# Attention and two gated layers on one core: the written-out order of instructions is made with later transfers, longer vector steps and new priorities

## The chip, the cores and the metric

The kernel runs on one core of a Trainium2 chip. The metric is the device time of one execution in microseconds, lower is better; three runs of the kernel before are given.

## What is computed

Block-causal attention over 4 batches, 8 heads, 576 positions and 64 features, then two layers of two products each, with an elementwise function between them. In the first layer the function is h * cos(h), in the second relu(h) squared.

```python
def _attn_ref(q, k, v):
    ...
    scores = scale * np.matmul(q, k.transpose(0, 1, 3, 2))
    mask = block_i >= block_j
    scores = np.where(mask, scores, -1000000000.0)
    scores = scores - np.max(scores, axis=-1, keepdims=True)
    attn = np.exp(scores)
    attn = attn / (np.sum(attn, axis=-1, keepdims=True) + 1e-09)
    return np.matmul(attn, v)
...
h = x @ w_in          # 2304 x 512 by 512 x 2048
g = h * np.cos(h)     # second layer: np.maximum(h, 0) ** 2
x = g @ w_out         # 2304 x 2048 by 2048 x 512
```

q, k and v are float32. The four weight matrices are 64-bit floats, so the kernel loads their 8-byte words and makes float32 of them itself.

## The kernel before

**The work.** The matmuls take float32 operands split in a high part (rounded for the matmul) and a low part (the rest); each product is then three matmuls: high by high, high by low, low by high (`mm3`). The high parts come from `hi_part`, the low parts from `lo_part`.

**The stages.** First attention by units of one batch and one pair of heads (`attention`: load, transposes of q and k in `prep`, scores, softmax, transposes of the result, product with v), together with the first half of the first layer's columns (`first_in`, `in_cos`, `first_out`) for groups of 256 and 320 tokens. Then three stages over chunks of 512 tokens (four chunks and a half one): the second half of the first layer, and the two halves of the second layer. Each chunk's input comes back from DRAM (tile x, from x_d or y_d, in `raw_rows`), sums of its quarters (tiles t) are made in `load_quarters`, and high and low parts xh and xl in `x_parts`. These stages multiply 256 x 256 blocks with seven products instead of eight (`quad`); the weights' seven combinations are made in `left_parts` (high and low part so, from ws or c), stored to DRAM as wi_d and loaded back as w in `factors`. The sums of products are kept in PSUM or in tiles p, u and r; the function's result is split into gh and gl, the operands of the second product (`y`). The results of half a layer go to DRAM (y1_d, y_d, y2_d) and are added in with the other half.

**The weights.** `weight_piece` (line 683) loads 128 x 512 words into a tile raw, of which there are two (`RAWS`, L694). ACT makes tiles t and c of their top bytes, DVE or POOL subtracts them, and DVE puts the middle bytes in (L430). This last step frees raw.

**The order.** Nothing is ordered by hand. Each step is recorded with a cost in ns, the tiles that it reads and writes, and the engines that may do it (`FREE` names the kinds with a choice: hi, lo, copy, norm, abs, wt, eps, add). `Recorder.schedule` (line 219) then plays the program through. Among the steps that are ready at an engine's free time, it takes the one with the lowest priority number, which is the step's place in the program plus an offset by kind and phase (`PUT_OFF`). A step with a choice goes to the engine that would end it first, with that engine's cost changed by a factor 1 + `BIAS` of the phase. Phase 0 is the first batch, phase 1 the other batches, phase 2 the second half of the first layer, phase 3 the second layer. The order that comes out is what each engine gets; on the chip it then works through it strictly in that order, waiting where an operand is not there yet.

Transfers are an engine of their own in it (`DMA`, issued from SP's queue, 500 ns apart): a transfer lands at line 319, and its readers are ready 50 ns later by line 328:

```python
o.end = landed = max(t + self.LANDING, landed) + o.service   # LANDING = 1750; service = size / 420, 2400 for raw
...
lat = 50 if e == "DMA" else self.LAT.get((e, a), 0 if a == e else 100)
```

The other handovers take `LAT`, 87 to 258 ns by pair of engines. On the chip a semaphore guards each of them, so the order has no bearing on what is computed.

Of the kernel before, what the change touches and what calls it, by code (L numbers as in the profile page):

```python
# [21 lines left out]

BANKS = {"h": 1, "y": 1, "s": 2, "t": 1, "a": 1}, {"h": 6, "y": 3, "s": 5, "t": 3, "a": 1}

BIAS = [{"DVE": 1.84, "ACT": 0.4, "POOL": 0.23}, {"DVE": 3.3, "ACT": -0.66, "POOL": -0.23}, {"DVE": 0.9, "ACT": -3.04, "POOL": -0.02}, {"DVE": -0.14, "ACT": -3.34, "POOL": 1.15}]

FREE = {"hi": "POOL ACT", "lo": "DVE POOL", "copy": "ACT DVE", "norm": "POOL DVE", "abs": "DVE", "wt": "POOL DVE", "eps": "ACT DVE", "add": "DVE POOL"}

# [8 lines left out]
NATB = 1  # L37


PUT_OFF = [{"load": -35, "weights": -24, "prep": 14, "scores": 25, "weighted": 9, "split": 279, "in": -32, "cos": -170, "out": -10, "warm": 9160, "later": 935}, {"load": 376, "weights": -150, "prep": -70, "scores": 69, "weighted": -156, "split": 84, "in": 43, "cos": -141, "out": -21, "later": 886}, {"load": 194, "weights": 721, "prep": 429, "scores": 43, "weighted": -280, "split": 374, "in": -36, "cos": -108, "out": -53, "later": 567}, {"in": 32, "out": 14, "later": 22}]  # L40

UPTO = [8, 12, 14, 16, 18]
NEG = -1000000000.0
# [10 lines left out]
class View:  # L54
    def __init__(self, vt, chain, ix, halves):
        self.vt, self.chain, self.ix, self.halves = vt, chain, ix, halves
# [83 lines left out]
class Recorder:  # L140
# [6 lines left out]
    }  # L147

    ISSUE, LANDING = 500, 1750

    def __init__(self):
        self.ops = []
# [18 lines left out]
    def any(self, alts, writes=(), reads=(), after=(), lat=0, holds=()):  # L171
# [6 lines left out]
        o.phase, o.kind = self.phase, self.kind  # L178
        o.prio = o.seq + PUT_OFF[self.phase].get(self.kind, 0)
        o.deps, o.outs, o.tiles = set(after), [], []  # L180
# [38 lines left out]
    def schedule(self):  # L219
        ops = self.ops  # L220
        engines = dict.fromkeys(e for o in ops for e in o.alts)
        for o in ops:
            for t in o.tiles:
                o.deps.update(getattr(t.pool, "after", ()))
                if t.banks is None and t.before is not None:
                    o.deps.update(t.before.users)
            o.ahead -= o.deps
            o.ahead.discard(o)
            o.left, o.ready = len(o.deps) + len(o.ahead), dict.fromkeys(o.alts, 0.0)
            for d in o.deps:  # L230
                d.outs.append(o)
            for d in o.ahead:
                d.behind.append(o)
        free = dict.fromkeys(engines, 0.0)
        free["DMA"] = 1850.0
        waiting = {e: [] for e in engines}
        ready = {e: [] for e in engines}

        def wait(o, at=0.0):
            for e in o.alts:  # L240
                heapq.heappush(waiting[e], (max(at, o.ready[e]), o.prio, o.seq))

        def finish(o, e, t):

            at = max(t, free[e], o.ready[e])
            at += sum(ops[s].alts[e][1] for p, s in ready[e] if p < o.prio and e in ops[s].alts)
            if e == "DVE" and len(o.alts[e]) > 3 and pool[1]:
                at = max(at, pool[0])
            return at + o.alts[e][1] * (1 + BIAS[o.phase][e])

        for o in ops:
            if not o.left:
                wait(o)
        order, done, gives, table, cold, busy = [], 0, [], None, True, 0.0
        pool, landed, ended = (0.0, False), 0.0, 0.0
        while done < len(ops):

            best = None
            for e in free:
                t = free[e]  # L260
                if not ready[e] and waiting[e]:
                    t = max(t, waiting[e][0][0])
                elif not ready[e]:
                    continue
                if best is None or t < best[0]:
                    best = (t, e)
            if gives and (best is None or gives[0][0] <= best[0]):
                at, _, _, x = heapq.heappop(gives)
                x.banks.give(x.tag, x.bank)
                for o in x.banks.blocked:  # L270
                    wait(o, at)
                x.banks.blocked = []
                continue
            t, e = best
            while waiting[e] and waiting[e][0][0] <= t:
                _, p, s = heapq.heappop(waiting[e])
                heapq.heappush(ready[e], (p, s))
            _, s = heapq.heappop(ready[e])
            o = ops[s]
            free[e] = max(free[e], t)  # L280
            if e not in o.alts:
                continue
            if len(o.alts) > 1:
                a = min(o.alts, key=lambda a: (finish(o, a, t), a != e))
                o.alts = {a: o.alts[a]}
                if a != e:
                    continue
            new = [x for x in o.tiles if x.banks is not None and x.bank is None]
            full = next((x.banks for x in new if not x.banks.fits(x.tag, len(new))), None)
            if full is not None:  # L290
                full.blocked.append(o)
                continue
            for x in new:
                x.bank = x.banks.take(x.tag)
            o.eng, o.cost, o.fn = o.alts[e][:3]
            o.port = o.alts[e][3] if len(o.alts[e]) > 3 else 0
            o.alts = {}
            if o.table and o.table != table:
                t, table = t + 1283, o.table
            if e == "PE":  # L300

                if t - ended > 2300:
                    cold = True
                if t - ended > 250:
                    busy = t
                if t - busy > 3400:
                    cold = False
                if cold:
                    o.cost *= 2
            if o.port and e == "DVE" and t < pool[0] and (pool[1] or o.port == 2):  # L310
                t = pool[0]
            o.begin = t
            o.end = t + o.cost
            if e == "PE":
                ended = o.end
            if e == "POOL":
                pool = (o.end, bool(o.port))
            if e == "DMA":
                o.end = landed = max(t + self.LANDING, landed) + o.service
            if o.hook:  # L320
                o.hook()
            free[e] = o.begin + self.ISSUE if e == "DMA" else o.end
            order.append(o)
            done += 1
            for x in o.outs:
                x.left -= 1
                for a in x.alts:
                    lat = 50 if e == "DMA" else self.LAT.get((e, a), 0 if a == e else 100)
                    x.ready[a] = max(x.ready[a], o.end + lat)
                if not x.left:  # L330
                    wait(x)
            for x in o.behind:
                x.left -= 1
                for a in x.alts:
                    x.ready[a] = max(x.ready[a], o.begin)
                if not x.left:
                    wait(x)
            for x in o.tiles:
                if x.banks is not None:
                    x.todo = getattr(x, "todo", len(x.users)) - 1  # L340
                    x.last = max(getattr(x, "last", 0.0), o.end)
                    if not x.todo:
                        heapq.heappush(gives, (x.last + 100, x.users[0].seq, x.bank, x))
        order.sort(key=lambda o: (o.begin, o.seq))
        return order
# [1067 lines left out]
```

## Time and profile before

| | us |
|---|---|
| median of 3 runs | 1039.64 |
| lowest and highest | 1037.94, 1040.03 |
| the profiled execution | 1038.25 |
| its span, first to last instruction | 1036.5 |

The profile is that of one execution. Its engines: PE is TensorE's matmuls, PEld its weight loads, DVE VectorE, ACT ScalarE, POOL GpSimd, SP the engine that issues all transfers. L and a number is a line of the kernel. A busy time is the union of the records of one engine; a wait is idle time of an engine, put down to the semaphore that came last. PEclk is the granted clock of TensorE as a share of 2.4 GHz; a transfer's time runs from issue to landing. In out<-in the names are those of the program's tiles.

### The profile page before, as it was taken

What the parts mean: (1) busy time and instruction counts of PE and PEld (TensorE: products, weight loads), DVE (VectorE), ACT (ScalarE), POOL (GpSimd) and SP (SyncE); (2) the same over time, 40 slices, a digit from 0 to 9 for tenths busy, and PEclk for the clock granted to TensorE, in tenths of its full rate; (3) what the DMA queues carried; (4) which work ended last, traced back from release to release, by engine and by line L of the source; (5) the groups of instructions that cost most, each with busy time, mean ns of one, the idle gap of its engine ahead of it and who ended that gap; (6) DMA issues with size and microseconds to landing.
All of it is one profiled execution on the core that took longest, in us unless ns stands there. A gap on an engine that the chain in (4) does not pass through costs nothing.

```text
span 1036.5 us, 18463 instructions
## 1 busy us (share of the span) xinstructions
PE 990.8 (96%) x6672; PEld 863.7 (83%) x6672; DVE 641.0 (62%) x1344; ACT 636.4 (61%) x1417; POOL 340.6 (33%) x412
## 2 busy tenths in 40 slices
PE   7779999999999999999999889999998999999998
PEld 5557887878888898989797779898987888988987
DVE  4765666666364446395897688856868285736432
ACT  7897678878898975464484747545655272504301
POOL 5584144567886766060664520000000000000000
PEclk8989999999999999999999999999999999999999
DMA  6644133455565375712445698315474553221111
GB/s 181 186 134 125 47 84 86 133 170 154 150 186 175 111 264 180 269 41 89 141 147 169 200 304 308 98 49 193 163 214 163 226 201 102 62 82 51 52 61 41
DMA packets 136507, 150.11 MB, mean 145 GB/s; under 512 B 70368, under 2 KB 102624, under 8 KB 136416
## 3 DMA queue, kind: packets, MB, share of 16 engines
q1 hardware_dynamic: 136416, 148.93, 45.6%
q8 instruction: 53, 0.87, 0.4%
q14 instruction: 38, 0.31, 0.1%
HBM read 99.09 MB, written 49.81 MB: 144 GB/s over the span
## 4 chain that ended last, share of the span: by engine, by line
PE 54%; DMA 15%; ACT 10%; POOL 8%; DVE 8%; issue 4%; SPq 0%; POOLq 0%; ACTq 0%; DVEq 0%
PE y L529 24%; PE h L529 18%; PE t L546 5%; DMA wi_d<-so 5%; PE a L539 4%; DMA x<-y_d 3%; PE s L539 2%; POOL xl L467 2%; DMA raw<-in_moe_w_in_dram 2%; DMA w<-wi_d 2%; POOL e L512 2%; ACT gh L453 2%; DMA x<-x_d 2%; DVE r L423 1%; ACT e L414 1%
## 5 line engine op out<-in xcount | busy, mean ns | idle before, releaser
L529 PE MATMUL h<-xh,w 128*128 128x256 f32 x1536 | 289.8, 284 | 5.0 <-ACT p L482 2.8
L529 PEld LDWEIGHTS h<-xh,w 128*128 128x128 f32 x1536 | 244.5, 192 | 9.1 <-ACT p L482 3.8
L529 PE MATMUL y<-gh,w 128*128 128x256 f32 (+2 forms) x832 | 213.6, 334 | 13.6 <-ACT gh L453 8.4
L529 PE MATMUL h<-xl,w 128*128 128x256 f32 x768 | 217.3, 283 | 0.0
L529 PE MATMUL y<-w,gh 128*128 128x512 f32 x576 | 185.0, 398 | 2.6 <-ACT gh L453 2.6
L529 PEld LDWEIGHTS y<-gh,w 128*128 128x128 f32 x832 | 144.0, 191 | 29.5 <-ACT gh L453 10.7
L529 PEld LDWEIGHTS h<-xl,w 128*128 128x128 f32 x768 | 147.4, 192 | 1.1
L529 PE MATMUL y<-gl,w 128*128 128x256 f32 (+2 forms) x416 | 136.4, 332 | 3.7 <-POOL gl L467 3.5
L529 PEld LDWEIGHTS y<-w,gh 128*128 128x128 f32 x576 | 107.9, 189 | 29.1 <-ACT gh L453 4.2
L453 ACT ACTIVATE gh<-r 128x512 fp32r<-128x512 f32 (+2 forms) x134 | 74.4, 558 | 67.2 <-DVE r L1291 32.5
L529 PE MATMUL y<-w,gl 128*128 128x512 f32 x288 | 113.6, 397 | 0.0
L956 DVE CUSTOM_DVE_ANT_0 e<-s,mask 128x384 f32<-128x384 f32 (+4 forms) x160 | 70.9, 479 | 43.9 <-PE s L539 36.6
L512 POOL TENSOR_SCALAR e<-e,st 128x384 f32<-128x384 f32 (+4 forms) x134 | 83.4, 637 | 44.1 <-DVE st L977 31.7
L529 PEld LDWEIGHTS y<-gl,w 128*128 128x128 f32 x416 | 79.3, 191 | 12.0 <-POOL gl L467 5.4
L414 ACT ACTIVATE e<-e,st 128x128 f32<-128x128 f32 (+4 forms) x144 | 82.9, 578 | 6.3 <-DVE st L956 4.2
L471 DVE TENSOR_TENSOR gl<-r,gh 128x512 fp32r<-128x512 f32 (+2 forms) x88 | 65.8, 752 | 15.0 <-ACT gh L453 11.8
L546 PE MATMUL t<-ident,e 128*128 128x128 f32 (+1 forms) x400 | 66.8, 284 | 7.5 <-POOL e L512 7.1
L423 DVE TENSOR_TENSOR o<-y,y 128x512 f32<-128x512 f32 (+1 forms) x38 | 25.1, 662 | 72.9 <-PE y L529 69.1
L467 POOL TENSOR_TENSOR gl<-r,gh 128x256 fp32r<-128x256 f32 (+2 forms) x60 | 56.2, 938 | 37.9 <-ACT gh L453 37.2
L482 ACT ACTIVATE p<-h 128x512 f32<-128x512 f32 x48 | 28.3, 589 | 64.2 <-PE h L529 64.2
L529 PEld LDWEIGHTS y<-w,gl 128*128 128x128 f32 x288 | 54.5, 189 | 13.8 <-DVE gl L471 1.1
L482 ACT ACTIVATE r<-t 128x384 f32<-128x384 f32 (+1 forms) x111 | 56.9, 532 | 13.0 <-PE t L546 12.0
(140 smaller groups left out, 1881.5 us busy)
## 6 DMA issues: line engine op xcount, KB each, us to landing
wi_d<-so SPq DMA_DIRECT2D x84, 256.0 KB, 2.7
w<-wi_d SPq DMA_DIRECT2D x42, 512.0 KB, 6.8
raw<-in_moe_w_in_dram SPq DMA_DIRECT2D x32, 512.0 KB, 5.2
raw<-in_moe_w_out_dram SPq DMA_DIRECT2D x32, 512.0 KB, 3.9
y<-y_d SPq DMA_DIRECT2D x34, 256.0 KB, 3.0
y_d<-o SPq DMA_DIRECT2D x34, 256.0 KB, 3.0
x<-y_d SPq DMA_DIRECT2D x16, 512.0 KB, 3.9
k<-in_k_dram SPq DMA_DIRECT2D x36, 128.0 KB, 3.0
```

The source lines that it names most:

```text
L414: return nc.scalar.activation(real(out), real(in_), func, **kw)
L423: out.size / 0.96 + 68, lambda: nc.vector.tensor_tensor(real(out), real(a), real(b), op=op), [out], [a, b],
L453: "ACT": ("ACT", n / 1.2 + 92, lambda: nc.scalar.activation(real(hi), real(x), ACTF.Copy)),
L467: lambda: nc.gpsimd.tensor_tensor(real(lo), real(x), real(f(hi)), op=ALU.subtract), 1,
L471: lambda: nc.vector.tensor_tensor(real(lo), real(x), real(f(hi)), op=ALU.subtract), 1,
L482: "ACT": ("ACT", n / 1.2 + 50, lambda: nc.scalar.activation(real(out), real(ps), ACTF.Copy)),
L512: lambda: nc.gpsimd.tensor_scalar(real(out), real(x), real(s), 1.0, op0=ALU.mult, op1=ALU.mult),
L529: lambda: nc.tensor.matmul(real(ps), lhsT=real(lhsT), rhs=real(rhs), start=start, stop=stop, skip_group_check=True),
L539: nc.tensor.matmul(real(ps), lhsT=real(l), rhs=real(r), start=start, stop=stop, skip_group_check=True)
L546: lambda: nc.tensor.transpose(real(out), real(in_), real(ident)[0:rows, 0:rows]), [out], [in_, ident],
L956: lambda: nc.vector.tensor_tensor_reduce(out=real(e), in0=real(ps), in1=real(m), scale=-1.0, scalar=BIG, op0=ALU.add, op1=ALU.min, accum_o ...
```

## The change

Three numbers are new in the order's model: the readers of a transfer are ready 2497 ns after line 319's landing instead of 50, every step on DVE, ACT or POOL takes 16 ns more, and every handover between two engines 4 ns more. All offsets (`PUT_OFF`) but three are new, and so are all twelve biases. No step, tile, buffer or cost formula is changed.

```diff
--- before.py
+++ after.py
@@ -22,7 +22,7 @@
 
 BANKS = {"h": 1, "y": 1, "s": 2, "t": 1, "a": 1}, {"h": 6, "y": 3, "s": 5, "t": 3, "a": 1}
 
-BIAS = [{"DVE": 1.84, "ACT": 0.4, "POOL": 0.23}, {"DVE": 3.3, "ACT": -0.66, "POOL": -0.23}, {"DVE": 0.9, "ACT": -3.04, "POOL": -0.02}, {"DVE": -0.14, "ACT": -3.34, "POOL": 1.15}]
+BIAS = [{"DVE": 1.89, "ACT": 0.46, "POOL": 0.26}, {"DVE": 2.58, "ACT": -0.56, "POOL": 0.68}, {"DVE": -0.3, "ACT": -2.99, "POOL": 0.29}, {"DVE": -1.17, "ACT": -3.72, "POOL": 2.36}]
 
 FREE = {"hi": "POOL ACT", "lo": "DVE POOL", "copy": "ACT DVE", "norm": "POOL DVE", "abs": "DVE", "wt": "POOL DVE", "eps": "ACT DVE", "add": "DVE POOL"}
 
@@ -37,7 +37,7 @@
 NATB = 1
 
 
-PUT_OFF = [{"load": -35, "weights": -24, "prep": 14, "scores": 25, "weighted": 9, "split": 279, "in": -32, "cos": -170, "out": -10, "warm": 9160, "later": 935}, {"load": 376, "weights": -150, "prep": -70, "scores": 69, "weighted": -156, "split": 84, "in": 43, "cos": -141, "out": -21, "later": 886}, {"load": 194, "weights": 721, "prep": 429, "scores": 43, "weighted": -280, "split": 374, "in": -36, "cos": -108, "out": -53, "later": 567}, {"in": 32, "out": 14, "later": 22}]
+PUT_OFF = [{"load": 114, "weights": -25, "prep": 11, "scores": 21, "weighted": -156, "split": 287, "in": 62, "cos": -140, "out": -54, "warm": 9160, "later": 877}, {"load": 381, "weights": -104, "prep": -71, "scores": 69, "weighted": -789, "split": 92, "in": 43, "cos": -127, "out": -24, "later": 911}, {"load": 543, "weights": 771, "prep": 52, "scores": 520, "weighted": 66, "split": 1698, "in": 0, "cos": -391, "out": -77, "later": 696}, {"in": 92, "out": 124, "later": -317}]
 
 UPTO = [8, 12, 14, 16, 18]
 NEG = -1000000000.0
@@ -147,6 +147,7 @@
     }
 
     ISSUE, LANDING = 500, 1750
+    LATE, SLACK, EXTRA = 2497, 4, 16
 
     def __init__(self):
         self.ops = []
@@ -310,7 +311,7 @@
             if o.port and e == "DVE" and t < pool[0] and (pool[1] or o.port == 2):
                 t = pool[0]
             o.begin = t
-            o.end = t + o.cost
+            o.end = t + o.cost + (self.EXTRA if e in ("DVE", "ACT", "POOL") else 0)
             if e == "PE":
                 ended = o.end
             if e == "POOL":
@@ -325,7 +326,7 @@
             for x in o.outs:
                 x.left -= 1
                 for a in x.alts:
-                    lat = 50 if e == "DMA" else self.LAT.get((e, a), 0 if a == e else 100)
+                    lat = self.LATE if e == "DMA" else self.LAT.get((e, a), 0 if a == e else 100) + (self.SLACK if a != e else 0)
                     x.ready[a] = max(x.ready[a], o.end + lat)
                 if not x.left:
                     wait(x)
```

## Rows read from the trace of the kernel before

**Rows 1.** The page's busy time, share of the span and instructions by engine
```profile
PE 990.8 (96%) x6672; PEld 863.7 (83%) x6672; DVE 641.0 (62%) x1344; ACT 636.4 (61%) x1417; POOL 340.6 (33%) x412
```

**Rows 2.** Busy time by stage: length, each engine, clock, DMA share, GB/s
```profile
0.00:104.00 104.00, 83.93 (x566) 62.43 (x567) 62.10 (x188) 84.37 (x209) 63.27 (x83) 0.93 0.59 156
104.00:390.00 286.00, 283.15 (x2225) 242.17 (x2224) 161.23 (x533) 241.71 (x642) 172.63 (x248) 1.00 0.48 143
390.00:520.00 130.00, 124.64 (x790) 114.43 (x789) 84.96 (x104) 67.77 (x128) 54.05 (x38) 0.99 0.43 145
520.00:630.00 110.00, 102.32 (x644) 91.46 (x644) 89.02 (x117) 73.32 (x138) 49.24 (x42) 0.98 0.66 217
630.00:850.00 220.00, 214.59 (x1353) 192.36 (x1352) 150.40 (x260) 116.19 (x211) 1.39 (x1) 0.99 0.52 175
850.00:1014.00 164.00, 163.45 (x996) 144.90 (x995) 86.84 (x135) 48.76 (x87) 0.00 (x0) 1.00 0.21 68
1014.00:1036.50 22.50, 18.74 (x111) 16.00 (x109) 6.50 (x10) 4.32 (x7) 0.00 (x0) 0.97 0.06 24
```

**Rows 3.** Waits of PE, 0 to 104 us: total, times, longest
```profile
PE t L546 <- POOL e L512: 5.5, 5, 1.5
...
PE y L529 <- POOL w L448: 3.7, 1, 3.7
...
PE h L529 <- POOL w L448: 1.8, 2, 1.5
```

**Rows 4.** Waits of PE, 390 to 1014 us
```profile
PE y L529 <- ACT gh L453: 10.9, 7, 3.1
...
PE h L529 <- ACT p L482: 2.8, 4, 1.3
```

**Rows 5.** Timeline, 391 to 397 us, ACT and PE: start, duration, idle before
```profile
391.64 0.63 ACT L453 ACTIVATE xh<-x 128x512 fp32r<-128x512 f32 x1 [3.58 <-DMA x<-x_d]
...
396.04 0.63 PE L529 MATMUL y<-gh,w 128*128 128x256 f32 x3 [2.25 <-ACT gh L453]
```

**Rows 6.** Timeline, 590 to 602 us, ACT and PE
```profile
590.67 0.63 ACT L453 ACTIVATE xh<-x 128x512 fp32r<-128x512 f32 x1 [5.88 <-DMA x<-y_d]
...
601.45 1.55 PE L529 MATMUL y<-gh,w 128*128 128x512 f32 x3 [3.08 <-ACT gh L453]
```

**Rows 7.** Timeline, 788 to 797 us, ACT and PE
```profile
788.48 0.42 ACT L453 ACTIVATE so<-ws 128x256 fp32r<-128x256 f32 x1 [2.92 <-DMA wi_d<-so]
...
791.04 0.63 ACT L453 ACTIVATE xh<-x 128x512 fp32r<-128x512 f32 x1 [2.14 <-DMA x<-y_d]
...
796.04 2.02 PE L529 MATMUL y<-w,gh 128*128 128x512 f32 x4 [2.21 <-ACT gh L453]
```

**Rows 8.** Timeline, 776 to 781 us, ACT and PE
```profile
776.24 0.42 ACT L453 ACTIVATE so<-c 128x256 fp32r<-128x256 f32 x1 [1.43 <-DMA wi_d<-so]
...
780.36 0.38 PE L529 MATMUL h<-xh,w 128*128 128x256 f32 x1 [1.33 <-ACT p L482]
```

**Rows 9.** The chain of waits at 585 us: start, duration, what
```profile
584.84 5.75 DMA x<-y_d
```

**Rows 10.** The page's DMA issues: KB each, median us to landing
```profile
wi_d<-so SPq DMA_DIRECT2D x84, 256.0 KB, 2.7
w<-wi_d SPq DMA_DIRECT2D x42, 512.0 KB, 6.8
```

**Rows 11.** Busy time in 4 us stretches after the stall of rows 6
```profile
600.00:604.00 4.00, 2.55 (x9) 2.26 (x10) 4.00 (x6) 3.23 (x6) 1.52 (x2) 0.70 0.98 376
604.00:608.00 4.00, 4.00 (x19) 3.43 (x18) 4.00 (x5) 3.10 (x7) 2.47 (x2) 0.88 0.95 314
```

**Rows 12.** Instructions by shape, DVE: busy us, mean ns
```profile
L430 DVE SCALAR_TENSOR_TENSOR s<-n,r 128x512 f32<-128x512 int32 x36 | 36.9, 1024 | 3.8 <-ACT n L414 3.6
```

**Rows 13.** Timeline of SP's queue in the start
```profile
56.76 19.04 SPq L694 DMA_DIRECT2D raw<-in_moe_w_out_dram  x5
```

## The prediction, made before the changed kernel was run

> **What bounds the kernel now.** I read the page's busy times first: TensorE (PE) works 990.8 of 1036.5 us, its weight loads run beside its matmuls, and no other engine passes 62% [rows 1]. So PE's stream of matmuls sets the time, and its 45.7 us of idle time, with what its clock loses after an idle stretch, is all that another order of the same instructions can win. The view of busy time by stage says where that idle time lies [rows 2]: the attention start (0 to 104 us) 104 − 83.93 = 20.1 us; 104 to 390 us 2.9 us; 390 to 1014 us (130 − 124.64) + (110 − 102.32) + (220 − 214.59) + (164 − 163.45) = 19.0 us; the end 3.8 us, which no order shortens much, since an addition and a store follow the last matmul.
>
> Then I asked what ended those waits. In the start PE waits for GpSimd (POOL): normalised scores e and weight parts w [rows 3]. After 390 us it waits almost only for ACT's gh, 10.9 us, and ACT's p, 2.8 us [rows 4]. The question is what made ACT late, so I read ACT's own timeline ahead of the four longest of these stalls. Each time ACT, which works strictly in its order, stands at a step that needs a transfer, with gh, the step before gh or p queued behind it: 3.58 us at xh for x from x_d, then PE idle 2.25 us [rows 5]; 5.88 us at xh for x from y_d, then 3.08 us [rows 6]; 2.92 us at so and 2.14 us at xh, then 2.21 us [rows 7]; 1.43 us at so for a store that frees its buffer, then 1.33 us [rows 8]. So nearly half of the late idle time, 8.9 of 19.0 us, has a transfer at its root that the order placed too early.
>
> **How wrong the order's model was.** The model lands a transfer at issue + 1750 ns + size/420 ns (line 319) and lets its users start 50 ns later (line 328). For the x load behind the second of those waits, 512 KB, with nothing ahead of it in the model's queue, that is 1.75 + 1.25 + 0.05 = 3.05 us after issue; the chain of waits shows 5.75 us [rows 9], so the model is short by 2.7 us. For 256 KB it gives 2.42 us, where stores of so take 2.7 us [rows 10]; for the copies w from wi_d (512 KB) 3.05 against a median of 6.8 [rows 10], some of which is queueing that the model counts too. With 2497 in place of 50, the model's landing is 5.5 us for 512 KB and 4.87 us for 256 KB: about right for loaded queues, 2 us too late for quiet ones. Row and rule can be weighed here. The Trainium skill, "DMA: Bandwidth & Descriptors", section "Anatomy of one DMA — SWDGE (gpsimd) path", fits about 2.0 us plus size over 436 GB/s (for GpSimd's path, while this kernel issues from SP): an estimate of 2.6 us for 256 KB, with which the 2.7 us agree, and 3.2 us for 512 KB, with which the 5.75 us do not.
>
> **The parts, costed.** No instruction is added or removed; steps move.
>
> 1. *Later landing (line 328).* A step that needs a transfer is placed 2.45 us later behind other ready work, so I let each of the four waits shrink by 2.45 us and PE's stall by no more than it was: 2.25 (all of rows 5) + 2.45 of 3.08 (rows 6) + 2.21 (rows 7, where two waits stand in series) + 1.33 (rows 8) = 8.2 us.
>
> 2. *The clock.* After the stall of rows 6 the granted clock falls, from 2.4 to 1.2 GHz for part of two 4 us stretches: means of 0.70 with PE busy 2.55 us and 0.88 with 4.00 us [rows 11]. That loses 0.30 × 2.55 + 0.12 × 4.00 = 1.2 us. The stages of rows 5 and rows 7 also stand below 1.00 in [rows 2]; estimating their falls at the same, three cost 3.7 us and go with the stalls. Upper end of 1 and 2: 11.9 us.
>
> 3. *What is late next.* When ACT is free sooner, VectorE (DVE) is the next in line: it is busy 4.00 of 4.00 us in both stretches of rows 11, and it writes r, which gh needs. I therefore take half of 11.9, 6.0 us; the ends are 0 (DVE is the limit everywhere) and 11.9.
>
> 4. *16 ns per vector step, 4 ns per handover.* 1344 + 1417 + 412 = 3173 steps [rows 1] become 50.8 us longer in the model and not at all on the chip. Against real misses 16 ns is little: DVE's s from n costs 512/0.96 + 68 = 601 ns in the model and 1024 ns in the trace [rows 12]. I take nothing; it is covered by idle time on DVE, ACT and POOL, and if that cover fails it shows within the ends of part 3.
>
> 5. *New biases.* POOL's grows in every phase (0.23 to 0.26, −0.23 to 0.68, −0.02 to 0.29, 1.15 to 2.36) and DVE's falls in three, so flexible steps (lo, wt, add, norm) leave POOL for DVE. Between 390 and 630 us POOL is busy 54.05 + 49.24 = 103 us and DVE idle 45.0 + 21.0 = 66 us [rows 2]. If half of POOL's 103 us moves and runs twice as fast, DVE gets 26 us more, with room on average and none where it is full. Both signs: I take nothing and 3 us either way.
>
> 6. *SP's queue and the weight loads.* All transfers stand in one queue, and one that waits holds up those behind it: five raw loads take 19.04 us there because each waits for a raw buffer (there are two) [rows 13]. Freeing a buffer comes 2.45 us later in the model, so loads of q, k and v are likely to be put ahead of raw loads: sooner attention, later weights. The start's 20.1 us can go either way. The nearest rows are 5.5 us for e and 3.7 + 1.8 us for w [rows 3]; I take nothing, with 5 us either way.
>
> Sum: −6.0 us against the profiled execution, 1038.25 us (span 1036.5 and 1.75 around it), so 1032.25. The median shown, 1039.64, is 1.39 above that execution, so on the median's footing 1033.6; I say 1033.5.
>
> **The rivals.**
>
> A. *Weights starve the start* (slower). Eight loads of w_in and eight of w_out pass through two raw buffers before the first stage can run on. A lap is 2.45 us longer in the model, the eight w_out loads make four laps in each buffer: 9.8 us later in the order. PE has 20.1 us of idle time there already, so it has nothing to fill with, and waits for w. The late gain of 6.0 us stays at best: 1033.5 + 9.8 = 1043; without half of it 1046. It decides once the last raw load of w_out is issued more than 6 us later than now (75.8 us, the end of rows 13). For it: PE waits for w already [rows 3]. Against it: what lands on the chip does not land later, and in the start ACT is busy 84.37 of 104 us [rows 2], so something useful is done in the meantime.
>
> B. *DVE takes the stall over* (no change). The steps that leave POOL fall on DVE where it is full [rows 11]; ACT's waits shrink, and r comes as late as before: 1038 to 1041. Against it: with less on POOL the 1024 ns of rows 12 should shrink as well.
>
> C. *A flat margin misses* (no change). Most transfers land by the old model, within 0.3 us for 256 KB [rows 10]; late are those on loaded queues. Then the order puts off steps that were in time by as much as it cures, the 6.0 us are given back, and the time is 1039.6. By the page's rule named above it would be this one; the 5.75 us speak against it.
>
> D. *The start gains too.* q, k and v ahead of raw loads save 5 us of the 20.1, and three quarters of part 3's 11.9 go: 1039.6 − 5 − 8.9 = 1025.7, down to 1022.7 with all of it.
>
> That nothing moves can't be: every step's readiness and priority changes.
>
> **How the numbers follow.** Forecast 0.48 (its own range 1027 to 1039, from the ends of part 3), A 0.26, B 0.10, C 0.06, D 0.10. About 0.2%, 2 us, is what a measurement can tell from no change. Faster: forecast and D, 0.58; same: B and C, 0.16; slower: A, 0.26. The range reaches from 1023 (D) to 1045 (most of A); left out are the tails of D and A.
>
> **What would show it.** Right: ACT's waits at xh and so for transfers are under 1 us between 390 and 1014 us, PE waits for gh there for less than 6 us, the three falls of the clock in that stretch are gone or fewer, and PE's idle time is near 40 us. Part 5: POOL's busy time falls between 390 and 630 us and DVE's rises. Wrong: PE idle over 24 us in the start, with waits for w in front and the last w_out load issued after 82 us (A); gh as late as before with ACT waiting for DVE (B); new waits of PE at steps that stood in time (C).

## The result and the profile after

The changed kernel takes 1003.38 us (median of 4 runs, 1002.99 to 1003.96) against 1039.84 for the kernel before on the same chip: a ratio of 0.9648, 95% interval 0.9626 to 0.967. That is 36 us faster where 6 were forecast, and outside the range. The profiled execution took 1003.07 us, its span is 1001.3.

The page's busy times, as in [rows 1]:

```profile
PE 978.8 (98%) x6672; PEld 862.2 (86%) x6672; DVE 663.3 (66%) x1469; ACT 636.6 (64%) x1423; POOL 203.6 (20%) x281
```

Busy time by stage, with the columns of [rows 2], the same stretches of time:

```profile
0.00:104.00 104.00, 86.75 (x577) 64.19 (x578) 65.55 (x186) 86.04 (x216) 59.18 (x84) 0.92 0.61 157
104.00:390.00 286.00, 285.50 (x2265) 248.77 (x2263) 188.67 (x605) 244.37 (x649) 119.59 (x175) 1.00 0.48 145
390.00:520.00 130.00, 129.82 (x860) 121.00 (x858) 92.68 (x153) 76.25 (x144) 9.06 (x9) 1.00 0.46 156
520.00:630.00 110.00, 109.15 (x726) 100.11 (x727) 92.35 (x153) 73.16 (x134) 15.74 (x13) 1.00 0.70 232
630.00:850.00 220.00, 220.00 (x1340) 196.08 (x1340) 153.26 (x265) 115.42 (x211) 0.00 (x0) 1.00 0.52 171
850.00:1001.30 151.30, 147.56 (x914) 132.09 (x912) 70.81 (x110) 41.34 (x72) 0.00 (x0) 1.00 0.19 59
```

After 390 us PE was idle for 19.0 us ahead of the end [rows 2]; now it is 0.2 + 0.9 + 0.0, and the last row's 3.7 us are the end, which was 3.8. The start kept most of its idle time, 17.3 us against 20.1. POOL lost 137 us of work, and DVE, which got more instructions (1469 for 1344), is busy for only 22 us more. PE's waits in the start, as in [rows 3] (total, times, longest, in us):

```profile
PE y L530 <- POOL w L449: 3.2, 2, 2.9
...
PE t L547 <- POOL e L513: 1.8, 3, 0.8
```

and from 390 us to the end, as in [rows 4]; these two are all there are:

```profile
PE y L530 <- DVE gl L472: 0.8, 2, 0.4
PE y L530 <- ACT gh L454: 0.2, 1, 0.2
```

The waits for x that preceded rows 5 to 7, from the view of the tile x (idle time, in us and times, that a load of x ended on any engine; then the time from issue to landing), before:

```profile
  DMA x<-y_d: 11.2, 7
  DMA x<-x_d: 10.8, 5
...
DMA to landing us min/median/max: 2.7/3.7/11.5
```

and after:

```profile
  DMA x<-x_d: 3.3, 3
  DMA x<-y_d: 0.4, 1
```

Among the waits of ACT for transfers after 390 us, so for wi_d was the largest before:

```profile
ACT so L453 <- DMA wi_d<-so: 24.6, 14, 5.6
```

After, it is down to a sixth:

```profile
ACT t L415 <- DMA raw<-in_moe_w_in_dram: 7.6, 3, 3.7
...
ACT so L454 <- DMA wi_d<-so: 3.9, 4, 2.5
```

DVE's steps of [rows 12], from 390 to 640 us (busy us, mean ns). Before, s from n had a mean of 1024 ns, and r from r and s:

```profile
L423 DVE TENSOR_TENSOR r<-r,s 128x512 f32<-128x512 f32 x36 | 35.5, 985 | 8.3 <-ACT s L414 8.2
```

After:

```profile
L431 DVE SCALAR_TENSOR_TENSOR s<-n,r 128x512 f32<-128x512 int32 x36 | 27.2, 756 | 3.8 <-ACT n L415 3.8
...
L424 DVE TENSOR_TENSOR r<-r,s 128x512 f32<-128x512 f32 x36 | 26.4, 732 | 6.0 <-ACT s L415 6.0
```

**Where the 35 us of span lie.** Both traces hold the same 6672 matmuls in other orders, so I lay them over each other by matmul work. Each matmul counts with the mean time from its start to the next one's start, for its names and shape, over the traces compared (the slowest twentieth left out); all together are 955 us. Then I read at what time each trace has done 75, 350 and all 955 us of work. Before, that was at 112.2, 400.4 and 1031.4 us, after at 110.7, 390.0 and 996.2. So 1.6 us were won in the start, 8.8 in the attention after it, and 24.8 after 350 us of work (the late part: the last of the attention and the three stages). The table gives this for every kernel that was run; a minus is a gain on the kernel before. The parts come from the profiled execution, the median from all runs. Where a kernel's runs spread, the two differ: the profiled execution is 5.3 us above the median for late50, 3.6 for before_jit and 2.3 for pool23, and 4.65 below it for bias23. bias23 and pool23 keep the order of the kernel before until about 394 us, so their start and attention, up to 1.9 us, show what one execution differs from another. The kernel before, timed beside each of them, had medians of 1037.8 to 1041.2 us, so rows are better compared by their ratios than by their medians.

| kernel | median us (lowest to highest) | ratio to before [95%] | start | attention | late |
|---|---|---|---|---|---|
| the change | 1003.4 (1003.0 to 1004.0) | 0.9648 [0.9626, 0.9670] | −1.6 | −8.8 | −24.8 |
| model_only | 1024.9 (1023.7 to 1025.9) | 0.9850 [0.9797, 0.9904] | +5.8 | −6.0 | −13.8 |
| draw_only | 1027.8 (1027.1 to 1028.3) | 0.9877 [0.9832, 0.9921] | +3.3 | +4.0 | −17.4 |
| oldbias | 1010.3 (1009.0 to 1011.1) | 0.9708 [0.9664, 0.9752] | −2.7 | −7.2 | −19.5 |
| oldput | 1012.0 (1011.2 to 1012.7) | 0.9725 [0.9681, 0.9769] | +5.7 | −6.0 | −26.4 |
| late50 | 1025.9 (1024.3 to 1031.3) | 0.9880 [0.9844, 0.9916] | +4.9 | −0.3 | −11.7 |
| no_extra | 1019.0 (1018.2 to 1019.6) | 0.9804 [0.9782, 0.9827] | +5.0 | −5.4 | −18.3 |
| bias23 | 1026.9 (1022.3 to 1032.2) | 0.9898 [0.9858, 0.9938] | +0.5 | −1.6 | −14.9 |
| jitter | 1007.9 (1007.5 to 1008.6) | 0.9699 [0.9677, 0.9721] | −1.3 | −4.4 | −25.0 |
| pool23 | 1027.3 (1024.8 to 1030.8) | 0.9887 [0.9851, 0.9922] | +1.0 | +1.9 | −11.9 |
| before_jit | 1036.4 (1032.1 to 1040.0) | 0.9972 [0.9950, 0.9994] | +3.3 | +1.1 | −2.9 |
| late3500 | 1019.1 (1017.6 to 1020.3) | 0.9808 [0.9779, 0.9838] | +6.7 | −5.9 | −21.2 |
| mix | 1002.4 (1002.3 to 1002.6) | 0.9645 [0.9623, 0.9667] | −1.0 | −8.9 | −25.8 |
| jitter2 | 1005.4 (1004.0 to 1005.7) | 0.9657 [0.9620, 0.9694] | −1.8 | −6.0 | −24.8 |
| latebias | 1021.3 (1020.3 to 1022.4) | 0.9814 [0.9782, 0.9846] | +10.8 | −4.8 | −22.1 |
| late1250 | 1007.3 (1006.2 to 1008.0) | 0.9678 [0.9647, 0.9709] | −1.1 | −6.0 | −25.0 |

### The profile page after: what moved, and what is told of

Same layout as the page of the kernel before. It is cut to its first block, busy times and chain, and to the rows that moved or that the text cites. A ratio compares the mean times of both kernels' runs of the same rounds, so it can differ in the third digit from the quotient of the medians.

```text
span 1001.3 us, 18384 instructions
## 1 busy us (share of the span) xinstructions
PE 978.8 (98%) x6672; PEld 862.2 (86%) x6672; DVE 663.3 (66%) x1469; ACT 636.6 (64%) x1423; POOL 203.6 (20%) x281
## 4 chain that ended last, share of the span: by engine, by line
PE 89%; DVE 4%; ACT 3%; POOL 2%; issue 1%; DMA 1%; SPq 0%; POOLq 0%; DVEq 0%
PE y L530 40%; PE h L530 35%; PE t L547 6%; PE a L540 4%; PE s L540 3%; PE s L530 1%; DVE c L431 1%; DVE s L431 1%; DVE r L424 1%; POOL e L513 1%; ACT e L415 1%; POOL c L717 1%; DVE gl L472 0%; DMA raw<-in_moe_w_in_dram 0%; ACT c L415 0%
## 5 line engine op out<-in xcount | busy, mean ns | idle before, releaser
L454 ACT ACTIVATE gh<-r 128x512 fp32r<-128x512 f32 (+2 forms) x138 | 76.6, 556 | 50.5 <-DVE r L1292 34.0
L472 DVE TENSOR_TENSOR gl<-r,gh 128x512 fp32r<-128x512 f32 (+2 forms) x135 | 85.7, 639 | 27.6 <-ACT gh L454 24.9
L957 DVE CUSTOM_DVE_ANT_0 e<-s,mask 128x384 f32<-128x384 f32 (+4 forms) x160 | 71.0, 478 | 30.4 <-PE s L540 22.1
L513 POOL TENSOR_SCALAR e<-e,st 128x256 f32<-128x256 f32 (+4 forms) x124 | 75.3, 621 | 75.3 <-DVE st L978 55.6
L483 ACT ACTIVATE r<-t 128x384 f32<-128x384 f32 (+1 forms) x110 | 56.1, 533 | 12.8 <-PE t L547 11.9
L530 PE MATMUL h<-xs2h,w 128*128 128x320 f32 x256 | 61.5, 313 | 0.0
```

What stands on the lines that cost most here:

```text
L454: "ACT": ("ACT", n / 1.2 + 92, lambda: nc.scalar.activation(real(hi), real(x), ACTF.Copy)),
L472: lambda: nc.vector.tensor_tensor(real(lo), real(x), real(f(hi)), op=ALU.subtract), 1,
L483: "ACT": ("ACT", n / 1.2 + 50, lambda: nc.scalar.activation(real(out), real(ps), ACTF.Copy)),
L513: lambda: nc.gpsimd.tensor_scalar(real(out), real(x), real(s), 1.0, op0=ALU.mult, op1=ALU.mult),
L530: lambda: nc.tensor.matmul(real(ps), lhsT=real(lhsT), rhs=real(rhs), start=start, stop=stop, skip_group_check=True),
L957: lambda: nc.vector.tensor_tensor_reduce(out=real(e), in0=real(ps), in1=real(m), scale=-1.0, scalar=BIG, op0=ALU.add, op1=ALU.min, accum_o ...
```

## The experiments

All of them compute the whole result; only the order differs. "Margin" is the landing of 2497 ns, "step times" are the 16 and 4 ns. Unless said otherwise a diff is against the changed kernel.

**The change in halves.** model_only has the model's numbers with the old offsets and biases:

```diff
-BIAS = [{"DVE": 1.89, "ACT": 0.46, "POOL": 0.26},
...
+BIAS = [{"DVE": 1.84, "ACT": 0.4, "POOL": 0.23},
...
-PUT_OFF = [{"load": 114, "weights": -25,
...
+PUT_OFF = [{"load": -35, "weights": -24,
...
```

> The model's three new numbers (2497, 4, 16) with the old offsets and biases. Theory M (transfers counted as later are what removes the stalls): most of the 36 us comes with them, 1003 to 1015 us, ACT's long waits for x and so after 390 us gone, POOL as busy as before (about 100 us between 390 and 630 us). Theory B (new biases take work off POOL and so off the port that DVE shares with it): little of it, 1030 us or more, and DVE's s from n still near 1 us. Theory D (offsets and biases are drawn for one model and fit no other): 1030 us or more, or slower than before.

draw_only has the new offsets and biases with the old model:

```diff
-    LATE, SLACK, EXTRA = 2497, 4, 16
+    LATE, SLACK, EXTRA = 50, 0, 0
```

> New offsets and biases with the old model (50, 0, 0). Theory M: the long waits of ACT for transfers stay, 1025 us or more. Theory B: POOL's busy time between 390 and 630 us falls to some 30 us, DVE's s from n to under 0.8 us, 1003 to 1015 us. Theory D: 1030 us or more.

Measured: 1024.9 and 1027.8 us. Neither theory alone holds, nor D. model_only, waits after 390 us:

```profile
ACT so L454 <- DMA wi_d<-so: 7.0, 8, 2.0
...
PE y L530 <- ACT gh L454: 3.1, 2, 1.6
...
PE h L530 <- DMA w<-wi_d: 2.5, 2, 2.0
```

ACT's waits at so fell from 24.6 to 7.0 us and PE's for gh from 10.9 to 3.1, as theory M had it; but two waits for w at the start of a stage are new, and DVE is nearly as slow as before:

```profile
L431 DVE SCALAR_TENSOR_TENSOR s<-n,r 128x512 f32<-128x512 int32 x36 | 33.4, 927 | 0.7 <-ACT n L415 0.7
```

draw_only is the mirror image. ACT waits for wi_d nearly as before, and PE still for gh and p:

```profile
ACT so L454 <- DMA wi_d<-so: 23.3, 18, 3.1
...
PE y L530 <- ACT gh L454: 3.7, 4, 2.3
...
PE h L530 <- ACT p L483: 2.7, 4, 1.0
```

yet its late part gained 17.4 us, more than model_only's 13.8. So there are at least two causes in the late part, and each alone brings more than half of the change's 24.8 us.

**One part undone.** oldbias is the change with the old biases:

```diff
-BIAS = [{"DVE": 1.89, "ACT": 0.46, "POOL": 0.26},
...
+BIAS = [{"DVE": 1.84, "ACT": 0.4, "POOL": 0.23},
...
```

> The change without the new biases. Theory M: within 6 us of the change, at most 1010 us. Theory B: most of the gain is lost, 1025 us or more, POOL near 100 us between 390 and 630 us. Theory D: 1015 us or more, by stalls in other places than before.

oldput is the change with the old offsets:

```diff
-PUT_OFF = [{"load": 114, "weights": -25,
...
+PUT_OFF = [{"load": -35, "weights": -24,
...
```

> The change without the new offsets. Theory M: within 6 us of the change, at most 1010 us. Theory B: the same, at most 1010 us, with POOL at some 30 us between 390 and 630 us. Theory D: 1015 us or more.

Measured: 1010.3 and 1012.0 us, both just past theory M's 1010 and short of D's 1015. oldbias keeps start and attention and loses 5.3 us of the late part; oldput keeps all of the late part and loses 10.1 us ahead of it. Its busy time by stage shows PE full from 390 us on, with the old offsets:

```profile
0.00:104.00 104.00, 83.15 (x529) 60.77 (x530) 57.48 (x161) 80.48 (x197) 59.92 (x81) 0.89 0.55 145
...
390.00:520.00 130.00, 130.00 (x863) 121.49 (x863) 87.15 (x146) 72.21 (x139) 5.99 (x5) 1.00 0.51 173
...
520.00:630.00 110.00, 109.92 (x742) 101.68 (x742) 94.67 (x158) 73.70 (x139) 16.32 (x11) 1.00 0.66 217
...
630.00:850.00 220.00, 219.66 (x1358) 196.39 (x1357) 159.46 (x275) 122.13 (x223) 0.00 (x0) 1.00 0.53 179
```

So the model's three numbers and the biases make the late part, and the offsets matter ahead of it.

**The model's numbers one by one.** late50 takes the margin away and keeps the step times:

```diff
-    LATE, SLACK, EXTRA = 2497, 4, 16
+    LATE, SLACK, EXTRA = 50, 4, 16
```

> The change with the landing put back to 50 ns, the 16 and 4 ns kept. Theory M (late stalls are those of transfers placed too early, together with POOL's use): like new offsets and biases alone (1027.8 us), 1022 to 1031, ACT's waits for wi_d back over 15 us after 390 us. Rival E (the 16 and 4 ns matter as much): 1012 us or less.

no_extra takes the step times away and keeps the margin:

```diff
-    LATE, SLACK, EXTRA = 2497, 4, 16
+    LATE, SLACK, EXTRA = 2497, 0, 0
```

> The change without the 16 and 4 ns, landing 2497 kept. Theory M: the late part stays free of stalls; in all 1003 to 1010 us. Rival E: 1015 us or more.

Measured: 1025.9 us for late50, as theory M said, and ACT's waits for wi_d are at 24.0 us again. no_extra, at 1019.0, is past the 1015 that rival E named, and theory M missed it: 6.5 us of the late part and 10.0 us ahead of it are lost. So the change needs the step times as well as the margin; without the margin they do not do it, where E had late50 at 1012 us or less. In the late part the loss is mostly in one place, the first matmuls of a stage, where PE waits between 600 and 660 us (the granted clock of 630 to 660 us is 0.94):

```profile
PE h L530 <- DMA w<-wi_d: 2.3, 1, 2.3
PE h L530 <- ACT xh L454: 0.9, 1, 0.9
```

**The biases alone.** bias23 is the kernel before with the new biases of phases 2 and 3, that is, the change with

```diff
-    LATE, SLACK, EXTRA = 2497, 4, 16
+    LATE, SLACK, EXTRA = 50, 0, 0
-PUT_OFF = [{"load": 114, "weights": -25,
...
+PUT_OFF = [{"load": -35, "weights": -24,
...
-BIAS = [{"DVE": 1.89, "ACT": 0.46, "POOL": 0.26},
...
+BIAS = [{"DVE": 1.84, "ACT": 0.4, "POOL": 0.23}, {"DVE": 3.3, "ACT": -0.66, "POOL": -0.23}, {"DVE": -0.3, "ACT": -2.99,
...
```

> The kernel before with the new biases of phases 2 and 3 alone: old model, old offsets. Until 350 us of matmul work the same order as before, so no difference there. Theory of two causes (POOL's slow steps and the port that it shares with DVE on one side, late transfers on the other): the part after 390 us gains 8 to 14 us, 1026 to 1032 us in all, DVE's s from n near 0.75 us, ACT's waits for wi_d still over 15 us. If transfers alone count: 1037 us or more. If POOL alone counts: 1018 us or less.

Measured: 1026.9 us; the late part gained 14.9 us, just above the 8 to 14 expected, in an execution that was the fastest of the four; s from n fell to 821 ns, and ACT's waits at so were still 18.3 us. Two causes again. Whether the biases' share is POOL's, pool23 tests, as a diff against the kernel before:

```diff
-{"DVE": 0.9, "ACT": -3.04, "POOL": -0.02}, {"DVE": -0.14, "ACT": -3.34, "POOL": 1.15}]
+{"DVE": 0.9, "ACT": -3.04, "POOL": 8.0}, {"DVE": -0.14, "ACT": -3.34, "POOL": 8.0}]
```

> The kernel before with POOL's bias at 8 in phases 2 and 3 and nothing else: POOL gets hardly a step after 390 us, DVE and ACT do its work. If POOL's steps are the second cause (they take twice DVE's time, and slow DVE's own steps while they run): DVE's s from n at 0.70 to 0.75 us against 1.02, 8 to 16 us off the part after 390 us, 1024 to 1032 us in all, although DVE gets more to do. If DVE's fill is the limit, as the prediction's part 3 and rival B had it: 1038 us or more.

Measured: 1027.3 us, 11.9 us off the late part. Among the DVE steps between 390 and 640 us, r from h and p took this before:

```profile
L423 DVE TENSOR_TENSOR r<-h,p 128x512 f32<-128x512 f32 x16 | 10.8, 681 | 12.6 <-PE h L529 12.6
```

With pool23 the steps of the same stretch are:

```profile
L430 DVE SCALAR_TENSOR_TENSOR s<-n,r 128x512 f32<-128x512 int32 x36 | 24.8, 688 | 2.6 <-ACT n L414 2.5
...
L423 DVE TENSOR_TENSOR r<-r,s 128x512 f32<-128x512 f32 x36 | 24.8, 689 | 6.1 <-ACT s L414 6.1
...
L423 DVE TENSOR_TENSOR r<-h,p 128x512 f32<-128x512 f32 x18 | 12.4, 688 | 12.4 <-PE h L529 12.4
```

and the busy time of the two stretches, in the columns of [rows 2]:

```profile
390.00:520.00 130.00, 125.86 (x815) 116.70 (x814) 82.03 (x137) 70.14 (x131) 8.91 (x11) 0.99 0.48 161
520.00:630.00 110.00, 107.21 (x700) 98.33 (x700) 90.11 (x163) 76.08 (x143) 0.00 (x0) 0.98 0.67 227
```

POOL's 103 us of [rows 2] are down to 9, their work is on DVE and ACT, and DVE is no busier than before: 82.0 + 90.1 us against 85.0 + 89.0. The steps that read two operands from SBUF, s from n and r and r from r and s, cost 1.02 and 0.99 us on average before, where POOL ran beside some of them, and 0.69 without it; r from h and p, with one operand in PSUM, cost 681 ns before and 688 here. The timeline of the kernel before shows it step by step. DVE (start, duration):

```profile
598.39 1.21 DVE L730 TENSOR_TENSOR t<-x 128x512 f32<-128x512 f32 x1
599.53 1.20 DVE L423 TENSOR_TENSOR r<-r,s 128x512 f32<-128x512 f32 x1
600.65 0.68 DVE L430 SCALAR_TENSOR_TENSOR s<-n,r 128x512 f32<-128x512 int32 x1
```

and POOL beside it:

```profile
597.89 1.17 POOL L729 TENSOR_TENSOR ws<-c,ws 128x256 f32<-128x256 f32 x1
599.33 0.86 POOL L467 TENSOR_TENSOR so<-c,so 128x256 fp32r<-128x256 f32 x1 [0.27 <-ACT so L453]
```

The first two DVE steps each end 0.54 us after a POOL step does (599.60 after 599.06, 600.73 after 600.19); the third, which is clear of POOL, takes 0.68. So a DVE step that meets POOL waits until POOL's is over and then does its work, and the wait counts as its busy time. All 46 steps of four kinds (s from n and r, r from r and s, gl, and t from x and t) that began while a POOL step ran, between 390 and 640 us, end 0.53 to 0.55 us after it. The Trainium skill, "SBUF — State Buffer", section "Who interferes with whom", says that a DVE instruction with two SBUF inputs contends with a GpSimd instruction that reads SBUF, that one with at most one such input, outside the two-port modes, does not, and that the lock on the ports they share is exclusive. The rows agree, down to the PSUM operand that spares DVE the wait (681 and 688 ns).

pool23 takes away POOL's own slower steps as well, and no run tells the two apart. Before, PE waited for such a step three times between 390 and 1014 us:

```profile
PE y L529 <- POOL gl L467: 2.9, 3, 2.2
```

**How much is luck.** jitter and jitter2 are differences without meaning:

```diff
-    LATE, SLACK, EXTRA = 2497, 4, 16
+    LATE, SLACK, EXTRA = 2490, 4, 16
```

> The change with 2490 in place of 2497, a difference without meaning, which changes the order of many steps all the same. How much an order moves by luck: within 2 us of the change if offsets and model matter by their size (1001 to 1006 us); 1008 us or more if the offsets fit this one number by chance.

```diff
-    LATE, SLACK, EXTRA = 2497, 4, 16
+    LATE, SLACK, EXTRA = 2504, 4, 16
```

> The change with 2504 in place of 2497, a second difference without meaning. With 2490 it took 1007.9 us (+4.5), all of it ahead of the late stages. If the offsets fit 2497 by a narrow chance: 1007 us or more again; if the change lies in a broad valley: 1001 to 1006 us. After 390 us PE stays free of stalls either way.

before_jit, against the kernel before:

```diff
-    ISSUE, LANDING = 500, 1750
+    ISSUE, LANDING = 500, 1757
```

> The kernel before with 1757 in place of 1750 for a transfer's landing, a difference without meaning. How much of the 36 us could be that the order before was an unlucky one: within 5 us of 1039.7 if it was not; 1030 us or less if it was.

Measured: 1007.9, 1005.4 and 1036.4 us. Seven nanoseconds cost the change 4.5 and 2.0 us by the medians (5.3 and 0.9 by the ratios, and jitter2's interval overlaps the change's), nearly all of it in the attention, and gain the kernel before 0.3% by the ratio; none touches the late part of the change. jitter lies just between the two bounds that were named, jitter2 where a broad valley would put it. By the one other order that was tried, the order before was not an unlucky one, and a few us of the 36 are the luck of the draw.

**More margin, and less.** late3500 and late1250:

```diff
-    LATE, SLACK, EXTRA = 2497, 4, 16
+    LATE, SLACK, EXTRA = 3500, 4, 16
```

> The change with 3500 ns in place of 2497. If a flat margin misses by holding back steps that are in time (rival C of the prediction), more of it costs: 1012 us or more, with new waits of PE after 390 us. If holding back costs nothing as long as engines have other work: the part after 390 us stays free of stalls, and the whole differs by the luck of the order, 1000 to 1011 us.

```diff
-    LATE, SLACK, EXTRA = 2497, 4, 16
+    LATE, SLACK, EXTRA = 1250, 4, 16
```

> The change with half the margin, 1250 ns. The rows put the old landing 0.3 us short for quiet queues and 2.7 us for loaded ones, so half of it should clear the quiet ones alone: ACT's waits for wi_d after 390 us between the 24 us of 50 ns and the 3.9 us of 2497, the late part between, 1008 to 1022 us in all. If the margin works as a threshold, it is like 50 ns: 1022 us or more.

Measured: 1019.1 and 1007.3 us. Half the margin does all that the whole does in the late part (−25.0), which neither of late1250's two expectations had; ACT's waits for wi_d come back to 10.0 us, but PE has work meanwhile. With 3500 the attention and most of the late part keep their gain (PE waits 2.5 us there, for w, xl and xh at a stage's start), and 6.7 us are lost in the start. Its last raw load of w_out is issued late (SP's queue; before, the last one ended its issue at 75.8 us):

```profile
83.36 0.33 SPq L695 DMA_DIRECT2D raw<-in_moe_w_out_dram  x1
```

**Without the step times and the new offsets.** latebias:

```diff
-    LATE, SLACK, EXTRA = 2497, 4, 16
+    LATE, SLACK, EXTRA = 2497, 0, 0
-PUT_OFF = [{"load": 114, "weights": -25,
...
+PUT_OFF = [{"load": -35, "weights": -24,
...
```

> The kernel before with the landing of 2497 and the new biases, without the 16 and 4 ns and without the new offsets. If the 16 and 4 ns matter in the late stages by themselves: the part after 350 us of matmul work gains under 20 us of the 26.5 that it had with them (old offsets, new biases, all three numbers: 1012 us), 1018 us or more in all. If that difference (1019 us for the change without them) was the fit of the offsets and one late w: 24 us or more there, 1009 to 1016 us in all.

Measured: 1021.3 us, but with a late part of −22.1, and in time it shows PE full there:

```profile
390.00:520.00 130.00, 129.98 (x856) 119.98 (x855) 86.38 (x142) 70.37 (x137) 12.49 (x10) 1.00 0.53 184
520.00:630.00 110.00, 108.38 (x719) 98.32 (x718) 93.10 (x151) 74.31 (x137) 21.82 (x18) 1.00 0.62 206
630.00:850.00 220.00, 219.90 (x1397) 198.30 (x1396) 161.63 (x282) 126.18 (x231) 0.00 (x0) 1.00 0.55 184
```

So the step times give 4.3 us of oldput's late 26.4. In all they are worth 9.3 us with the old offsets (1012.0 with them), 15.6 with the new ones (no_extra). The loss of latebias is in the start, +10.8 us, the worst of all, with the last raw load of w_out issued at 89.8 us. The expectation tied the whole time to the late part and is wrong in that; the 22.1 lie between its two bounds.

**Putting the best parts together.** mix has the old offsets in phases 2 and 3:

```diff
-{"load": 543, "weights": 771, "prep": 52,
...
+{"load": 194, "weights": 721, "prep": 429,
...
```

> The change with the old offsets in phases 2 and 3, the new ones in 0 and 1. Without new offsets the part after 350 us of matmul work gained 26.5 us, with them 24.8, and the part ahead of it 0.2 against 10.4. If the parts add up: 1000 to 1004 us, no slower than the change. If offsets must fit across the parts: 1008 us or more.

Measured: 1002.4 us, the parts add up. It is the fastest kernel of all, by 1.0 us of the median and with no run above the change's fastest, though the two were not timed side by side and their ratios to before overlap.

## Why the prediction was wrong

**The sign and the first mechanism were right.** Transfers that land later than the order thought did block ACT, all four stalls of rows 5 to 8 went, and the clock's falls after 390 us with them (PEclk is 1.00 in every stretch). ACT's waits at xh are down to 1.0 us, those at so to 3.9, where under 1 was foretold. But the sum was 6.0 us and the span fell by 35.2. The steps that failed are parts 3, 4 and 5, which halved the gain and put two terms at nothing, and the size of part 1.

**Part 5 failed.** It took the biases at nothing, with 3 us either way, since what POOL loses DVE must do. pool23 alone gains 11.9 us in the late part; taken out of the change, the biases are worth 6.9 us, 5.3 of them there (oldbias). The evidence stood in the rows: the 1024 ns of rows 12 were read as an error of the model that 16 ns could not mend, and rival B's own text said that they should shrink with less on POOL, but no price was put on it. Nor are the 601 ns all that the model counts: the line `if o.port and e == "DVE"`, which stands in the context of the diff, starts such a DVE step only once POOL's is over. And of PE's late waits the prediction named ACT's gh and p and passed over the 2.9 us for POOL's gl, which are longer than those for p. 36 steps of each of two kinds, 0.34 and 0.30 us apiece, are 23 us of DVE time, nearly as much as the 26 us of moved work that part 5 feared. In the change 78 of POOL's 103 us between 390 and 630 us left it, and DVE's busy time rose by 11.

**Part 3 failed with it.** It halved the gain because DVE was busy 4.00 of 4.00 us after the stall of rows 6. Much of that time was not work: in those 8 us four of its steps ran beside POOL and took 1.20 to 1.78 us instead of 0.68, and so did four in a row just ahead of them, where r and gl were made for the stalled matmuls (1.21 to 1.22 us each). Busy time on one engine held waiting for another. The chain of waits that ends in the stall of rows 6 runs through these steps (start, duration, what):

```profile
595.03 1.15 DVE r L423
...
599.53 1.22 DVE r L423
600.76 0.64 ACT gh L453
```

Five such steps start 1.14 to 1.15 us apart there, against 0.61 for two that are clear of POOL (at 603.28 and 603.89 us). By the four distances, an estimate of some 2 us of that stall's 3.08 was POOL's, where the prediction put it all down to the transfer. With the biases, little was late next: the model's numbers and the biases together gave 26.4 us (oldput), where 8.2 + 3.7 had been the upper end.

**Part 1 was too small as well.** It priced four stalls. The model's three numbers with nothing else new (model_only) gave 13.8 us in the late part in spite of two new waits for w, and 6.0 in the attention, where the prediction saw 2.9 us of idle time and looked no further; what the 2497 ns give alone was not run. That is the first paragraph's error: idle time and clock are not all that an order can win. A matmul's record is longer than its turn, as the kernel before shows in a dense stretch (start, duration):

```profile
682.02 0.28 PE L529 MATMUL h<-xl,w 128*128 128x256 f32 x1
682.14 0.40 PE L529 MATMUL h<-xh,w 128*128 128x256 f32 x2
682.38 0.28 PE L529 MATMUL h<-xl,w 128*128 128x256 f32 x1
```

Starts are 0.12 us apart and a record is 0.28 long, so a delay of up to 0.16 us between two matmuls leaves no idle time. Of the 35.2 us of span 23.2 were idle time (45.7 to 22.5). The other 12.0 are PE's busy time, which fell from 990.8 to 978.8 with the same matmuls; by the mean clock (0.988 of 1036.5 us, 0.991 of 1001.3) an estimate of 3.4 us of that is the clock's. The rest, over 8 us, was lost between matmuls.

**Part 4** took nothing for the step times. It nearly stands in the late part (latebias has 22.1 of oldput's 26.4 us without them), and fails in the whole: without them the change takes 1019.0 us and not 1003.4, and by the parts 10.0 us of the loss lie ahead of the late part. With the old offsets it is 6.3 there (latebias against oldput). Why the step times matter there is not shown.

**Part 6 and rival A** had the start right in part and wrong as a forecast. The new model with the old offsets does cost it 5.8 us (model_only), with the last raw load of w_out issued at 85.0 us, past the 82 that rival A named, though PE is idle there for 21.1 us and not for more than 24. The new offsets undo that; in the change it is issued at 81.3 us, and the start gains 1.6. Every kernel past 83 us lost 5 us or more in the start. late50, draw_only and before_jit lost 4.9, 3.3 and 3.3 without being late there, so this is not the only way to lose there, and that the late raw loads are the cause was argued, not tested. The granted clock is another. Over the first 104 us it is 0.93 before [rows 2]; in draw_only and no_extra (in this order) PE is idle there for less time than before, and the clock is 0.87:

```profile
0.00:104.00 104.00, 85.78 (x537) 62.58 (x538) 60.32 (x175) 83.36 (x205) 64.80 (x87) 0.87 0.58 152
0.00:104.00 104.00, 84.89 (x523) 60.25 (x523) 62.75 (x184) 86.27 (x213) 55.34 (x75) 0.87 0.56 149
```

0.06 of some 85 us is an estimate of 5 us, about what these two lost. late3500 and latebias have 0.93 and 0.92 there, and PE idle for 22.3 and 23.5 us.

**Rival D** had the size of the start wrong, 1.6 us where it wanted 5; what went beyond the forecast came from the late part and the attention.

**Rival B** had the work of POOL fall on a full DVE; with pool23 it did, and DVE was busy for 172.1 us between 390 and 630 us where it had been 174.0.

**Rival C** is refuted for the late part: −11.7 at 50, −25.0 at 1250, −24.8 at 2497, −21.2 at 3500. What lies between 50 and 1250 was not run; past 1250 more margin gains nothing there, and at 3500 it costs at the stages' first w. The 5.75 us of rows 9 were slower than most: loads of x land after 3.7 us in the median, and 1250 ns put the model's landing at 4.25. What a too large margin costs is mostly in the start; that nothing else is there to do was argued, not tested.

Open: why the offsets fit the start only together with all three numbers (no_extra loses 5.0 us there for 20 ns, by the clock as far as the rows go), which would take a study of that order step by step.

## What to carry to other kernels

An order made by a model should treat a transfer as landing late: in the late stages, where the engines had other work, holding its readers back cost nothing up to 2497 ns, and half of that did as well. The size is not free: 3500 ns cost 15.7 us by the medians, more than half of it where the pipeline fills, and there the old priorities did not fit the new model. Before calling an engine full, compare its mean step with that of the same shape where the others are idle: here two kinds of DVE steps lost about a third of their time to waits beside POOL, and DVE got no busier when it took POOL's work over. And look for lost time between matmuls by their starts, not by PE's idle time.

## What was not expected of the hardware

A DVE step of 128x512 with both operands in SBUF took 0.69 us alone. One that began beside a POOL step ended 0.55 us after that step, and so took up to 1.79 us, all of it shown as busy; 1.02 us is the mean of both sorts in the kernel before. And the spread between runs differs: the four runs of each kernel with a margin of 1250 ns or more lie within 0.4 to 2.7 us of each other, while without it late50, bias23 and pool23 spread over 7.0, 10.0 and 6.0 us and before_jit, in ten runs, over 7.9; draw_only, with 1.3, is the exception. Why is not shown.
